# Half of the last half's convolution as matmuls, output blocks leaving from a key buffer, and a new order of the whole program

## The chip, the cores and the metric

The kernel runs on one core of one Trainium2 chip. The core has five engines with queues of their own: TensorE (PE), VectorE (DVE), ScalarE (ACT), GpSimd (POOL) and SyncE (SP), and 16 DMA engines. The metric is the device time in microseconds (us) of one execution; lower is better. The time before is the median of six runs.

## The reference

Block-sparse attention (blocks of 32, window, first and last block global, three random blocks a row), whose output is the input of a gated feed-forward layer with a depthwise convolution of three taps along the sequence. There are 4 batches of 768 tokens, 8 heads of 64, and a hidden width of 1024.

```python
scores = np.where(mask, scale * q @ k.T, -1e9)          # mask: window, global and sampled blocks
attn_out = softmax(scores) @ v                          # (4, 8, 768, 64) -> x (4, 768, 512)
h = np.maximum(x @ w_in, 0.0)                           # (4, 768, 1024)
hp = pad(h, one zero row at each end of the sequence)
for k in range(3):
    conv_out += conv_w[k][None, None, :] * hp[:, k:k + S, :]
gate = 1.0 / (1.0 + np.exp(-conv_out))
return h * gate @ w_out                                 # (4, 768, 512)
```

## The kernel before

**Halves and pairs.** The work is cut into eight halves `n`, each 384 tokens of one batch, and every half into four pairs of heads `hp`. For each pair, `attention` writes three score tiles into PSUM (two `st` tiles, L1003 to L1057), ScalarE takes the exponentials (L1021, L1046, L1064), one A.V step multiplies them with the values (67 matmuls, L1104), VectorE divides by the row sums (L1115, L1116), TensorE transposes (L1127), and ScalarE or VectorE copies the result into `xT` (L1134 or L1136).

**Feed-forward.** When all four pairs of a half are in `xT`, eight groups of four matmuls make x @ w_in (L1270, called f1 in what follows), each into one of four PSUM tiles `mix`; ScalarE or VectorE writes the relu into `hE` (L1281 or L1283). Two relu chunks make one convolution unit, so a half has four units, `a` = 0 to 3. A unit is done in one of two ways:

- `conv`, on VectorE: six taps (L1184), two adds (L1191), tanh on ScalarE (L1199), +1 (L1202), product with h into `gT` (L1211).
- `conv_pe`, on TensorE: six matmuls with diagonal matrices `dg` into an `st` tile (L1231), tanh on ScalarE straight from PSUM (L1240), +1 (L1243), product (L1246). Before, this is unit 2 of every half.

The diagonal matrices are made by GpSimd, six multiplications of the identity by a column of the taps (L687). A small patch (L1301 to L1308) mends the column where two halves of a batch meet.

**Output.** `out_block(n, c)` multiplies one third of a half's `gT` by w_out: eight matmuls of 512 columns in four pairs, one for each unit (L1154). One copy brings the block to a staging tile `o2s` (L1162 on ScalarE, L1164 on VectorE; three such tiles), and SP sends its 256 KB out (L1167). The third block of an even half waits for the patch, so it is written together with the odd half's blocks.

**Keys and values.** GpSimd issues the loads of q, k and v (L704, L791). Keys are transposed on TensorE (L733), evicted (L744, L746), and the sampled key blocks are copied into one of two key buffers `kg` (L913, VectorE and GpSimd). Values are rearranged on VectorE (L802) and written to a scratch tensor `vs` in DRAM by SP (L812); from there whole rows return into `vn` (L823) and the sampled rows into `vg`, by SP (L932) or by indirect DMAs of GpSimd (L923), eleven gathers a half. `vd` holds copies of the corner blocks of v (L842) and `kd` the global key blocks (L769).

**What sets the order.** Nothing above runs in the order of the source. Each step is an operation of a `Plan`: it has a priority (a due time), the engines that may do it with a cost each, its inputs, and the buffers that it takes from a pool or uses. `forward` builds an order for all five queues from these, `backward` makes new priorities from it, and `worth` gives the order a value by replaying it with jittered costs. `run` repeats this; it then changes the priorities at random, 200 times, and keeps the best order found. Which of two engines does an eviction is decided in the same search. The instructions are then written out in that order, and each engine works through its queue in turn.

Of the kernel before, what the change touches and what calls it, by code (L numbers as in the profile page):

```python
# [8 lines left out]
FP32 = mybir.dt.float32  # L9
# [60 lines left out]
PAGE, FETCH, FIRST = 256, 4.2, 63  # L70
LANES = 8
COLD_AFTER, COLD_FOR, REPLAYS = 2.2, 4.0, 6


class Plan:


    def __init__(self):
        self.ops = []
        self.pools = []  # L80

    def pool(self, n):
        p = Pool_(n)
# [3 lines left out]
    def op(self, alts, fn, prio, deps=(), lat=None, dma=None, mode=None, alloc=(), uses=(), earliest=0.0,  # L87
           after=(), lazy=False, n=0, nd=1, slack=0.0, gap=None):
        o = Op(alts, fn, prio, [d for d in deps if d is not None], lat, dma, mode, earliest)
        o.key = len(self.ops)  # L90
        o.lazy = lazy
        o.n = n
        o.nd = nd
        o.slack = slack
        o.gap = gap
        o.after = [d for d in after if d is not None]
        for b in alloc:
            o.allocs.append(b)
            b.users.append(o)
        for b in uses:  # L100
            o.uses.append(b)
            b.users.append(o)
        self.ops.append(o)
        return o
# [294 lines left out]
    def run(self, passes=6, trials=200):  # L399

        shake = random.Random(2)
        prio = [o.prio for o in self.ops]
        best = None
        for x in range(passes):
            order, span = self.forward(prio, x == 0)
            span = self.worth(order) if REPLAYS else span
            if best is None or span < best[0]:
                best = (span, list(prio), x == 0)
            prio = self.backward()
        for x in range(trials):  # L410
            prio = [p + shake.gauss(0.0, 1.0) for p in best[1]]
            for y in range(3):
                try:
                    order, span = self.forward(prio, False)
                except RuntimeError:
                    break
                span = self.worth(order) if REPLAYS else span
                if span < best[0]:
                    best = (span, list(prio), False)
                prio = self.backward()  # L420
        order, span = self.forward(best[1], best[2])
        return order
@with_exitstack
def kernel(
# [11 lines left out]
    nc = tc.nc  # L436
# [11 lines left out]
    QE, VE = 22.0, 34.0  # L448
    GAP, NGAP = 0.0, 1
    NSP = (5, 6, 7, 7, 7, 7, 7, 8)  # L450
    PEC = (2,)

    sb = ctx.enter_context(tc.tile_pool(name="sb", bufs=1))
    ps = ctx.enter_context(tc.tile_pool(name="ps", bufs=1, space=bass.MemoryType.PSUM))
# [72 lines left out]
    def t_act(n):  # L527
        return 0.07 + n / 1200.0
# [10 lines left out]
    def TS(s):  # L539
        return 12.0 + 2.5 * s if s < 4 else 22.0 + 5.0 * (s - 4)  # L540
# [603 lines left out]
    he_buf, he_m, gt_buf, gt_m, gate, relus = {}, {}, {}, {}, {}, {}  # L1144
    patch = {}

    def out_block(n, c, due, deps):
        b, g = divmod(n, 2)
        ob, mb = Buf(P_os), Buf(P_mix)
        prev = None  # L1150
        for a in range(4):
            def fn(e, a=a):
                for ffc in (2 * a, 2 * a + 1):
                    nc.tensor.matmul(out=mix_t[mb.index], lhsT=gT_t[gt_buf[n].index][:, ffc, 128 * c:128 * c + 128],  # L1154
                                     rhs=woutb[:, ffc, :], start=(ffc == 0), stop=(ffc == NFFC - 1),
                                     skip_group_check=True)
            prev = op({"PE": 2 * t_mm(512)}, fn, due + 0.2 * a, [prev, wout_ld[a // 2]] + deps[a], mode="F",
                      alloc=[mb] if a == 0 else [], uses=[gt_buf[n]] + ([mb] if a else []), n=4)

        def ev(e):  # L1160
            if e == "ACT":
                nc.scalar.copy(out=o2s_t[ob.index], in_=mix_t[mb.index])  # L1162
            else:
                nc.vector.tensor_copy(out=o2s_t[ob.index], in_=mix_t[mb.index])  # L1164
        evo = op({"ACT": t_act(512), "DVE": t_dps(512)}, ev, due + 1.5, [prev], alloc=[ob], uses=[mb])
        t0 = 384 * g + 128 * c
        sp(lambda e: nc.sync.dma_start(out=out[b, t0:t0 + 128, :], in_=o2s_t[ob.index]), due + 2.5, [evo], 0.75, uses=[ob], slack=0.0 if n == NHALF - 1 else 4.0)  # L1167

    last_cv = [None]
    last_mark = {}  # L1170
# [80 lines left out]
    for n in range(NHALF):  # L1251
# [12 lines left out]
        for ffc in range(NFFC):  # L1264
            hb = Buf(P_mix)
            due = base + W * 0.5 * ffc / 8

            def f1(e, ffc=ffc, hb=hb, n=n):
                for fc in range(NFC):
                    nc.tensor.matmul(out=mix_t[hb.index][:, 0:384], lhsT=winb[:, fc, 128 * ffc:128 * ffc + 128],  # L1270
                                     rhs=xT_t[xt_buf[n].index][:, fc, :], start=(fc == 0), stop=(fc == NFC - 1),
                                     skip_group_check=True)
            f_op = op({"PE": 4 * t_mm(384)}, f1, due, [win_ld[ffc // 4], he_m[b]] + [xtr[(n, hp)] for hp in range(4)], mode="F",
                      alloc=[hb], uses=[xt_buf[n]], n=8)

            def rl(e, ffc=ffc, hb=hb, b=b, g=g):
                dst = hE_t[he_buf[b].index][:, ffc, 1 + 384 * g:385 + 384 * g].rearrange(
                    "f (n r c) -> f n r c", r=4, c=8)
                src = mix_t[hb.index][:, 0:384].rearrange("f (n c r) -> f n r c", c=8, r=4)
                if e == "ACT":  # L1280
                    nc.scalar.activation(out=dst, in_=src, func=AF.Relu, bias=0.0, scale=0.5)  # L1281
# [78 lines left out]
```

## Time and profile before

| | us |
|---|---|
| median of six runs | 248.95 |
| range of the six runs | 247.27 to 252.5 |
| the profiled execution, its own time | 249.46 |
| its span in the profile | 247.6 |
| mean granted TensorE clock | 0.922 of full |

The page is one profiled execution: busy time of each engine, the span in 40 slices, the chain of work that ended last, and groups of instructions by source line. The time of the execution is 1.86 us longer than its span. Where the text speaks of a step of an instruction, it is the distance from one start to the next in an unbroken run of that instruction, which is shorter than the duration shown, because neighbours overlap.

### The profile page before, as it was taken

The numbers are of one execution on the slowest core, as the hardware profiler recorded it, in microseconds if no ns is written. First come the engines' busy times: TensorE is split into PE (matmuls) and PEld (weight loads), VectorE is DVE, ScalarE is ACT, GpSimd is POOL, SyncE is SP. The second block draws the span as 40 slices with busy tenths as digits, with TensorE's granted clock in tenths as the row PEclk, the third lists the DMA queues.
The fourth block names the chain that finished last, engine by engine and source line by source line (L and its number), as shares of the span: only waits on it lengthen the run. The fifth ranks groups of instructions, "written<-read, shape, count | busy, mean of one in ns | idle before, by whom it ended". The sixth has DMA issues, their size and how long they took to land.

```text
span 247.6 us, 10802 instructions
## 1 busy us (share of the span) xinstructions
PE 197.1 (80%) x4105; PEld 136.3 (55%) x4121; DVE 181.0 (73%) x657; ACT 171.9 (69%) x298; POOL 104.1 (42%) x203
## 2 busy tenths in 40 slices
PE   5233689497798499799869989699599999987792
PEld 1223577356465366668656755567376756645430
DVE  6545365378699958369998993769996984795882
ACT  8732858457578587779967985868587777865741
POOL 8068478870778791075388600753522000000000
PEclk9655758979999979999997999999999999999999
DMA  6949929999797369895519966674004412200113
GB/s 92 204 121 225 208 33 216 252 230 192 221 208 160 81 107 210 266 243 134 84 35 202 249 173 230 112 158 104 16 14 93 144 25 99 76 3 21 68 42 127
DMA packets 31687, 33.90 MB, mean 137 GB/s; under 512 B 4636, under 2 KB 27476, under 8 KB 31636
## 3 DMA queue, kind: packets, MB, share of 16 engines
q0 software_dynamic: 13600, 14.93, 35.3%
q1 hardware_dynamic: 17628, 17.89, 25.1%
q8 instruction: 32, 0.52, 0.9%
q10 hardware_dynamic: 408, 0.40, 0.6%
q14 instruction: 19, 0.16, 0.2%
HBM read 35.12 MB, written 9.62 MB: 181 GB/s over the span
## 4 chain that ended last, share of the span: by engine, by line
DVE 28%; PE 28%; DMA 13%; POOL 10%; issue 10%; ACT 6%; DVEq 1%; POOLq 1%; SPq 1%; ACTq 0%
PE mix L1154 10%; DVE m L1184 9%; DVE m L1191 5%; PE mix L1270 5%; POOL vg L923 5%; DMA vs<-vr 4%; PE mix L1104 3%; DMA vst<-in_v_dram 3%; DMA vg<-vs,idx 3%; DMA hE<-in_k_dram 3%; DVE xtok L1116 3%; PE st L1057 2%; DVE kg L913 2%; DVE gT L1211 2%; PE st L1039 2%
## 5 line engine op out<-in xcount | busy, mean ns | idle before, releaser
L1154 PE MATMUL mix<-woutb,gT 128*128 128x512 bf16 x176 | 45.6, 386 | 8.7 <-DVE gT L1211 5.7
L923 POOL DMA_INDIRECT vg<-vs,idx x34 | 33.9, 997 | 36.0 <-PE mix L1104 16.6
L1270 PE MATMUL mix<-xT,winb 128*128 128x384 bf16 x256 | 48.5, 341 | 0.5 <-DVE xT L1136 0.5
L1184 DVE TENSOR_SCALAR m<-hE,cw 128x384 bf16<-128x384 bf16 x144 | 36.0, 319 | 8.2 <-ACT hE L1281 8.1
L1281 ACT ACTIVATE hE<-mix 128x384 bf16<-128x384 f32 x56 | 27.7, 495 | 11.9 <-PE mix L1270 11.6
L1270 PEld LDWEIGHTS <-winb 128*128 128x128 bf16 x256 | 25.2, 101 | 16.8 <-issue 3.7
L913 DVE COPY kg<-kt 128x128 bf16 x192 | 26.6, 214 | 6.1 <-issue 6.0
L1046 ACT ACTIVATE pg<-st 128x736 bf16<-128x736 f32 x32 | 25.2, 788 | 7.7 <-PE st L1039 6.6
L1154 PEld LDWEIGHTS <-gT 128*128 128x128 bf16 x192 | 17.1, 99 | 23.5 <-DVE gT L1211 6.8
L1064 ACT ACTIVATE pr<-st 128x704 bf16<-128x704 f32 x32 | 24.4, 761 | 8.1 <-PE st L1057 7.8
L1104 PE MATMUL mix<-vg,pr 96*32 96x65 bf16 x704 | 26.3, 198 | 0.0
L1104 PE MATMUL mix<-vs,pa 128*32 128x65 bf16 (+1 forms) x320 | 25.8, 198 | 0.0
L1191 DVE TENSOR_TENSOR m<-m 128x768 bf16<-128x768 bf16 x48 | 25.6, 553 | 0.1
L913 POOL COPY kg<-kt 128x128 bf16 x72 | 20.4, 330 | 12.6 <-DVE kt L746 5.5
L1104 PE MATMUL mix<-vd,pg 128*32 128x130 bf16 x352 | 24.3, 227 | 0.8 <-POOL vd L842 0.8
L1199 ACT ACTIVATE m<-m 128x768 bf16<-128x768 bf16 x24 | 20.1, 848 | 5.2 <-DVE m L1191 5.1
L1104 PE MATMUL mix<-vn,pa 96*32 96x65 bf16 (+1 forms) x384 | 23.0, 199 | 0.0
L1104 PEld LDWEIGHTS <-pg 128*32 128x32 bf16 x736 | 21.5, 98 | 2.2 <-issue 1.5
L1104 PEld LDWEIGHTS <-pr 96*32 96x32 bf16 x704 | 21.6, 98 | 1.9 <-issue 1.6
L1104 PEld LDWEIGHTS <-pa 128*32 128x32 bf16 (+1 forms) x704 | 21.1, 97 | 2.4 <-issue 2.2
L1057 PE MATMUL st<-qb,kg 128*128 128x64 bf16 x352 | 16.8, 197 | 5.3 <-POOL kg L913 2.5
L1021 ACT ACTIVATE pa<-st 128x320 bf16<-128x320 f32 x32 | 14.0, 437 | 9.8 <-PE st L1012 8.8
(111 smaller groups left out, 420.0 us busy)
## 6 DMA issues: line engine op xcount, KB each, us to landing
out_dram<-o2s SPq DMA_DIRECT2D x24, 256.0 KB
vg<-vs SPq DMA_DIRECT2D x162, 32.5 KB
vn<-vs SPq DMA_DIRECT2D x8, 390.0 KB
vs<-vr SPq DMA_DIRECT2D x14, 195.0 KB
vst<-in_v_dram POOLq DMA_DIRECT2D x7, 384.0 KB, 7.4
nat<-in_k_dram POOLq DMA_DIRECT2D x12, 192.0 KB, 5.0
nat<-in_q_dram POOLq DMA_DIRECT2D x12, 192.0 KB, 4.8
winb<-in_moe_w_in_dram POOLq DMA_DIRECT2D x2, 512.0 KB
```

The lines of the kernel that those rows point to most:

```text
L913: eng.tensor_copy(out=dst[:, :, x, 32 * s:32 * s + 32], in_=KT[kt_buf[b].index][:, :, bass.ds(block_off(e, i0 + x, s, True), 32)])
L923: nc.gpsimd.indirect_dma_start(out=VG[vg_buf[n].index][:, x, :], out_offset=None, in_=vs_t[b][:, :], in_offset=bass.IndirectOffsetOnAxis(a ...
L1046: nc.scalar.activation(out=pg_t[pg.index], in_=st_t[sg.index][:, 0:736], func=AF.Exp, bias=0.0, scale=0.125)
L1057: nc.tensor.matmul(out=st[:, 64 * x:64 * x + 64].rearrange("p (h s) -> p h s", h=2), lhsT=kg[:, o:o + 128], rhs=qcol(i), start=True, stop= ...
L1064: nc.scalar.activation(out=pr_t[pr.index], in_=st_t[sr.index][:, 0:704], func=AF.Exp, bias=0.0, scale=0.125)
L1104: nc.tensor.matmul(out=dst, lhsT=l_, rhs=r_, start=(y == 0), stop=(y == len(lists[j]) - 1), skip_group_check=True)
L1154: nc.tensor.matmul(out=mix_t[mb.index], lhsT=gT_t[gt_buf[n].index][:, ffc, 128 * c:128 * c + 128], rhs=woutb[:, ffc, :], start=(ffc == 0), ...
L1184: nc.vector.tensor_scalar(out=mv(dst)[:, y], in0=hE_t[heb.index][:, f0 + y, c0 + tp_:c0 + tp_ + cn], scalar1=cw[:, tp_, f0 + y:f0 + y + 1] ...
L1191: nc.vector.tensor_tensor(out=m[:, 0], in0=m[:, 0], in1=m[:, x], op=ALU.add)
L1199: th = op({"ACT": t_act(W)}, lambda e: nc.scalar.activation(out=m_t[cb.index][:, 1], in_=m_t[cb.index][:, 0], func=AF.Tanh, bias=0.0, scal ...
L1270: nc.tensor.matmul(out=mix_t[hb.index][:, 0:384], lhsT=winb[:, fc, 128 * ffc:128 * ffc + 128], rhs=xT_t[xt_buf[n].index][:, fc, :], start= ...
L1281: nc.scalar.activation(out=dst, in_=src, func=AF.Relu, bias=0.0, scale=0.5)
```

## The change

Four things change. In the last half (`n` = 7) unit 3 also goes through `conv_pe`, so two of its four convolution units are matmuls; `dg` grows from six to twelve diagonal matrices, and GpSimd makes the second six in an operation that may not start before 130 on the planner's clock. The last four output blocks (three of half 7, and the third of half 6) are copied into a key buffer `kg` instead of `o2s`. The buffer is taken once, by a mark due when attention has ended, and each block has a 2 KB slot of it in every partition. The search of the order no longer adds a random number to the priority of all operations in a trial, but only to those whose priority lies in one stretch of 40 us, with a wider spread, from another seed; of 500 trials, 18 listed ones are worked out. The order of every queue comes out of that search, so it differs from before throughout the program.

```diff
+WIDTH, SIGMA = 40.0, 4.0
+SEED, TRIALS, KEEP = 1, 500, (0, 2, 5, 7, 11, 16, 27, 47, 48, 50, 81, 84, 95, 135, 197, 234, 350, 396)
...
-        shake = random.Random(2)
+        shake = random.Random(SEED)
...
-        for x in range(trials):
-            prio = [p + shake.gauss(0.0, 1.0) for p in best[1]]
-            for y in range(3):
+        for x in range(TRIALS):
+            lo = shake.uniform(-30.0, best[0])
+            prio = [p + shake.gauss(0.0, SIGMA) if lo <= p <= lo + WIDTH else p for p in best[1]]
+            for y in range(3 if KEEP is None or x in KEEP else 0):
...
-    PEC = (2,)
+    PEC = (2, 3)
+    ONPE = [(2,)] * 7 + [(2, 3)]
...
-        dg_ops[a_] = op({"POOL": 2.0}, mkdg, TS(3) + 0.1 * z, [cw_op, i_sel])
+        dg_ops[a_] = op({"POOL": 2.0}, mkdg, TS(3) + 0.1 * z if z == 0 else 120.0, [cw_op, i_sel], after=list(dg_ops.values()),
+                         earliest=0.0 if z == 0 else 130.0)
...
+    kg_late = Buf(P_kg)
+    kg_late_m = pl.mark(kg_late, TS(4 * NHALF))
+
     def out_block(n, c, due, deps):
         b, g = divmod(n, 2)
-        ob, mb = Buf(P_os), Buf(P_mix)
+        late = n == NHALF - 1 or (n == NHALF - 2 and c == 2)
+        ob, mb = kg_late if late else Buf(P_os), Buf(P_mix)
+        slot = c if n == NHALF - 1 else 3
+
+        def o2s():
+            if late:
+                return KG[ob.index][:, 1024 * slot:1024 * slot + 1024].bitcast(FP32)
+            return o2s_t[ob.index]
...
-                nc.scalar.copy(out=o2s_t[ob.index], in_=mix_t[mb.index])
+                nc.scalar.copy(out=o2s(), in_=mix_t[mb.index])
...
-        evo = op({"ACT": t_act(512), "DVE": t_dps(512)}, ev, due + 1.5, [prev], alloc=[ob], uses=[mb])
+        evo = op({"ACT": t_act(512), "DVE": t_dps(512)}, ev, due + 1.5, [prev] + ([kg_late_m] if late else []),
+                 alloc=[] if late else [ob], uses=[mb] + ([ob] if late else []))
...
-            if b not in WHOLE and ffc % 2 == 1 and ffc // 2 in PEC:
+            if b not in WHOLE and ffc % 2 == 1 and ffc // 2 in ONPE[n]:
                 conv_pe(n, ffc // 2, due + 1.5, relus[n][ffc - 1:ffc + 1])
```

More of the change, by code (lines that the diff above doesn't have):

```diff
@@ L80, in __init__ @@
         self.pools = []
+        self.kept = []
     def pool(self, n):
@@ L397, in worth, with run @@
         return sum(self.replay(order, random.Random(100 + x)) for x in range(REPLAYS)) / REPLAYS
-    def run(self, passes=6, trials=200):
-        shake = random.Random(2)
+    def run(self, passes=6):
+        shake = random.Random(SEED)
         prio = [o.prio for o in self.ops]
@@ L419, in run @@
                     best = (span, list(prio), False)
+                    self.kept.append(x)
                 prio = self.backward()
@@ L1161, in ev @@
             if e == "ACT":
-                nc.scalar.copy(out=o2s_t[ob.index], in_=mix_t[mb.index])
+                nc.scalar.copy(out=o2s(), in_=mix_t[mb.index])
             else:
-                nc.vector.tensor_copy(out=o2s_t[ob.index], in_=mix_t[mb.index])
-        evo = op({"ACT": t_act(512), "DVE": t_dps(512)}, ev, due + 1.5, [prev], alloc=[ob], uses=[mb])
+                nc.vector.tensor_copy(out=o2s(), in_=mix_t[mb.index])
+        evo = op({"ACT": t_act(512), "DVE": t_dps(512)}, ev, due + 1.5, [prev] + ([kg_late_m] if late else []),
+                 alloc=[] if late else [ob], uses=[mb] + ([ob] if late else []))
         t0 = 384 * g + 128 * c
-        sp(lambda e: nc.sync.dma_start(out=out[b, t0:t0 + 128, :], in_=o2s_t[ob.index]), due + 2.5, [evo], 0.75, uses=[ob], slack=0.0 if n == NHALF - 1 else 4.0)
+        sp(lambda e: nc.sync.dma_start(out=out[b, t0:t0 + 128, :], in_=o2s()), due + 2.5, [evo], 0.75, uses=[ob], slack=0.0 if n == NHALF - 1 else 4.0)
     last_cv = [None]
```

## The prediction, written before the changed kernel was run

> **What bounds the kernel now.** I read the page's totals first: is one engine full?
>
> ```profile
> PE 197.1 (80%) x4105; PEld 136.3 (55%) x4121; DVE 181.0 (73%) x657; ACT 171.9 (69%) x298; POOL 104.1 (42%) x203
> ```
>
> None is, so the order on the queues sets the time. The chain that ended last agrees; TensorE and VectorE have equal shares:
>
> ```profile
> DVE 28%; PE 28%; DMA 13%; POOL 10%; issue 10%; ACT 6%; DVEq 1%; POOLq 1%; SPq 1%; ACTq 0%
> ```
>
> Next, stages. The first w_in product (L1270) of a half is a milestone: it starts at 48.6 us for half 0, 106.9 for half 2, 164.6, 187.6, 211.0 and 227.1 for halves 4, 5, 6, 7 (the L1270 instructions by window). Busy time between the last of these:
>
> ```profile
> 187.60:211.00 23.40, 22.85 (x479) 15.82 (x477) 16.69 (x57) 18.50 (x34) 0.35 (x1) 1.00 0.32 95
> 211.00:227.10 16.10, 13.89 (x293) 9.01 (x293) 14.41 (x43) 10.39 (x19) 0.00 (x0) 1.00 0.06 20
> 227.10:243.60 16.50, 13.99 (x72) 6.78 (x71) 11.62 (x39) 9.72 (x17) 0.00 (x0) 1.00 0.12 48
> ```
>
> Columns after the length: PE, PEld, DVE, ACT, POOL, clock, DMA. Half 5's stage is TensorE alone (22.85 of 23.40); after 211 it is not full. The chain there is VectorE's convolution:
>
> ```profile
> 229.79 2.85 DVE m L1184 x12
> 232.64 1.40 DVE m L1191 x3
> ...
> 237.26 1.38 DVE m L1184 x6
> ...
> 239.61 0.57 DVE m L1191
> ...
> 240.20 0.85 ACT m L1199
> ...
> 241.47 0.57 DVE gT L1211
> ...
> 242.09 1.48 PE mix L1154 x6
> ```
>
> TensorE waits for gates; VectorE itself once waited long for relus:
>
> ```profile
> DVE m L1184 <- ACT hE L1281: 3.2, 1, 3.2
> PEld L1154 <- DVE gT L1211: 3.0, 4, 1.3
> ```
>
> No row has an output copy waiting for a staging buffer's DMA: ACT's L1162 waits only for L1154.
>
> **The Trainium skill.** "VectorE: DVE Perf Modes", section on the perf-mode tier table, puts bf16 tensor_scalar in a 4x mode and tensor_tensor in 2x. The trace agrees in kind: a 384-wide tap steps at 1.38/6 = 0.23 us, a 768-wide add at 0.47. "TensorE: Matmul & The Clock Gate", section on the HAM clock gate, says that an idle array falls to half clock and needs about 3.4 us of work to recover. The trace agrees: eleven L1057 take 0.74 us at 25.6 us and 0.48 at 38.8, so a new hole costs TensorE twice. "Perfetto Trace Analysis", section on identifying performance opportunities, says bottlenecks change between regimes; the table above does that.
>
> **The change, part by part.**
>
> *Third convolution unit of half 7 to TensorE.* Removed on VectorE: six taps, 1.38, and two adds, 2 x 0.47: 2.3 us of queue time. The +1 (L1243 for L1202) and gate product stay; ACT's tanh from PSUM is 0.81 instead of 0.85. Added on TensorE: six L1231, which step at the 0.163 us of L1270 (32 in 5.2 us): 1.0 us. It needs a score tile; both are free, attention being over.
>
> *Six more diagonal matrices on POOL.* 6 x 0.71 = 4.2 us, placed behind half-5 input loads, with part of those loads and two rounds of value gathers behind it. Taken as 0 to +1.5 us; I use 0, since POOL is 42% busy and input loads there run well ahead.
>
> *Last four output blocks in a key buffer.* Same copy (0.59 on ACT, 0.69 on VectorE), same 256 KB, same SP issue (0.37). No present wait is removed and the key buffer was last read long before: nothing, -0.3 to +0.3. After the last copy (244.23) the end at 247.6 stays 3.4 us away.
>
> *New order.* Every queue changes, so this is most of the risk. By the changed program's order, VectorE takes five more of the 24 output copies, and six value-corner copies (0.22 each) come from POOL. Net of the other moves VectorE gets about +1.8 us of work, ACT +0.3, TensorE +1.0. SP sends the first vn load ahead of the first three gathers (each 0.37 of issue) and not behind them; three key evictions move to ACT at the start (0.80 there, 0.56 on VectorE); both hide in ACT's wait until 22.4 for the first q transposes (8.1). Three stages I worked through:
>
> (a) Start. The first two A.V products need all eleven gathers of half 0. Now POOL issues its six at 20.3 to 28.2, a kd copy behind them waits until 32.24 for them to land, and A.V starts at 33.2. After: all four q loads come first, five gathers run from about 20.9 to 27, then a vd copy waits for those five (about 31.3), and only then the sixth is issued, landing some 3.5 to 4.8 later (the present one 4.8): 35.5 to 37. Behind that vd copy on POOL stand the sixth gather, another vd copy, both w_in loads (0.8 each), nine key copies (2.2) and the v loads of batch 1. A.V starts about 3 us late, and cold. But VectorE's normalisation of pair 3 now stands behind a copy that waits for a v load until 46.38, and TensorE idles 3.24 us before 48.07. That load is now issued at 38.4; after, at 31.3 + 0.5 (vd) + 1.3 (gather) + 0.5 (vd) + 1.7 (w_in) + about 0.5 (register work) + 2.2 (key copies) + 1.3 (one gather of half 1, now behind it) = 39.3, with the w_in transfers a us ahead of it and earlier than now. So it lands within about a us of now, and A.V's 3 us fit into this hole: f1 of half 0 moves by -0.5 to +1.5; I use +0.3.
>
> (b) Half 5's stage, full on TensorE. Counting matmuls at their steps (L1270 0.163, L1154 0.215, an A.V set of 67 0.85, an L1057 set 0.32, an L1008 to L1039 score set 0.75) gives 22.2 us now and 21.0 after: one A.V set and one score set have left. Half 4's stage gets 2.3 more, but has 3 idle; half 3's gets 2.0 less. I take -1.2, from -2.5 to +2.
>
> (c) Halves 6 and 7, from 211.0 to the last matmul at 243.6: 32.6 us now. I walked the new order by hand with the durations above. Half 6's 32 L1270 with one score set (5.2 + 0.75) and half 7's first A.V (0.85) make 6.8. From that point: A.V sets of pairs 1 and 2 (to 1.7), L1231 x6 (2.7), L1057 (3.0), exponential on ACT 0.76 (3.8), A.V of pair 3 (4.8). VectorE does four adds first (to 3.6), two xT copies, and normalises pairs 2 and 3 at 0.75 each with a +1 of 0.3 between (6.05); transposes and xT copy follow (0.35 + 0.5): half 7's f1 can start at 6.95. Half 6's last output blocks hold two of four mix banks, so relus pace L1270: the third relu on ACT stands behind a tanh that waits for VectorE's second add of half 6's last unit (10.65), and comes at 12.0. With 16 L1154 ahead of and between them, half 7's f1 ends at 15.7; L1231 x12 end at 17.7 (16.6 is the last relu). Then 32 L1154 x 0.215 = 6.9 run nearly without a hole (gates at 17.6, 19.1, 20.1, 21.0), to 24.9 with 0.3 of gaps. 6.85 + 24.9 = 31.7: -0.9. The 2.3 us taken from VectorE don't all come out, since **TensorE is late next**: it issues all 32 last L1154 after half 7's convolutions. The walk has no stall for instruction fetch: -2 to +1.5.
>
> Sum: +0.3 - 1.2 - 0.9 = -1.8. The profiled execution took 249.46, 1.86 more than its span of 247.6, so it becomes 247.7. It stands 0.5 above the median of the six runs (248.95); from the median, 247.15.
>
> **Rivals.** 0.5% is 1.25 us, about what a measurement of this kernel can tell from no change.
>
> *A, likeliest: TensorE's stages get shorter, as summed.* For: half 5's stage has no slack, and both walked stages end sooner. Against: counted by these steps TensorE works 158 of the 195 us from 48.6 to 243.6, so 37 us are holes, which a new order can fill or widen. 247.2; own range 245.0 to 248.5.
>
> *B, the end gains in full.* If the order also closes VectorE's 3.2 us wait for relus and TensorE's 3.7 us for gates (the waits of 211 to 244 have L1154 wait 2.1 us for L1211 and 1.6 for L1308), the unit's 2.3 us come out whole beside (b), with up to 1.5 more: 248.95 - 1.2 - 2.3 - 1.5 = 244. Against: the 6.9 us block of L1154.
>
> *C, slower: the sixth gather.* The vd copy on POOL holds that gather back. It decides once it lands later than about 37: the 3.2 us hole before 48.07 is then used up, and winb, v loads and later gathers behind it on POOL move too. Landing at 39 with a cold array: +2 in (a), and what POOL loses returns in the half-2 gathers, where the chain lies on it (62 to 79 us): +1 to +2. Less 1.2 for (b): 251. For: its slot is behind a drain of five gathers. Against: q loads and vn arrive sooner.
>
> *D, no change.* VectorE's extra 1.8 us of output copies, in stages where it is near TensorE (21.9 of 24.1 us from 106.9 to 131), eat the gain: 248.95 - 1.8 + 1.8 = 249.
>
> *E, the change doesn't do what it says.* The order does show twelve L1231 ahead of the last L1154 and four copies into kg, so only the size is open.
>
> **Chances.** A 0.40, B 0.17, C 0.23, D and E 0.20. Of A some 0.08 ends within 0.5%; of D about 0.06 ends slower and 0.03 faster. Faster: 0.32 + 0.17 + 0.03 = 0.52; slower 0.23 + 0.06 = 0.29; within 0.5%: 0.19. The time is A's 247.2. The range reaches down to B's 244 and its unknown (b), 243.5, and up to C's 251.
>
> **What would show it.** Right: f1 of half 0 starts within 1.5 us of 48.6; the stage from half 5's f1 to half 6's is about 22 us; from half 6's f1 to the last matmul about 31.7; L1231 runs 54 times, L1184 138; the last 32 L1154 stand without holes over 0.5 us. Wrong: f1 of half 0 after 50.5 (C); half 5's stage not shorter; VectorE still last on the chain before the final L1154 (gate later than the 26th of 32). Over 249 with both walked stages shorter means the loss is in halves 1 to 4, which I only counted.

## The result and the profile after

The changed kernel takes **249.24 us** (median of 26 runs, 245.26 to 252.41); the kernel before, run beside it on the same chip, 251.01 (55 runs, the six of the table above among them). The ratio is **0.9909, interval [0.9876, 0.9941]**: 0.9% faster, 2.3 us of 251. It is made from the fast runs alone, those within 1.5% of the fastest of their kernel, so it is not quite the ratio of the two medians, 0.9930. The prediction's 247.15 for 248.95 was a ratio of 0.9928. The sign and the size were right. One of its two gains was not where it was put.

Two profiles of the changed kernel are used. In the first one (its execution took 250.98 us) half 4's stage ran at a granted clock of 0.88, so figures for the whole span come from the second (248.36 us, span 246.6). The last three stages are shown from the first, since TensorE had full clock there, as it had before. Lines moved with the edits: f1 is L1288 (was L1270), the w_out matmul L1171 (L1154), taps L1202 (L1184), adds L1209, relu L1299, gate L1229, diagonal matmul L1249 (L1231), an A.V product L1111 (L1104), the last scores L1064 (L1057) with their exponential L1071, normalisation L1122 and L1123, transposes L1134.

First the page of the second profile, totals and then the chain by engine:

```profile
PE 197.0 (80%) x4108; PEld 136.3 (55%) x4127; DVE 184.2 (75%) x661; ACT 171.6 (70%) x294; POOL 103.9 (42%) x201
...
PE 52%; DVE 18%; DMA 10%; issue 7%; ACT 4%; SPq 3%; POOL 2%; POOLq 1%; DVEq 1%; ACTq 0%
```

TensorE's and VectorE's shares of the chain were equal, 28% each; now TensorE alone has half of it. VectorE's busy time did not fall: eight instructions left in half 7, but the output and corner copies that moved there more than replace them, and the same 192 copies into `kg` took 28.6 us where they took 26.6.

Busy time by stage, first profile: half 5, half 6, half 7, each from its first f1 product to the next (the last to the end of the last matmul). Columns after the length are PE, PEld, DVE, ACT, POOL, clock, DMA share, GB/s:

```profile
190.86:212.08 21.22, 21.01 (x388) 14.03 (x391) 17.21 (x56) 16.99 (x32) 0.00 (x0) 1.00 0.24 65
212.08:228.75 16.67, 12.92 (x354) 9.12 (x352) 10.38 (x34) 10.04 (x18) 0.00 (x0) 1.00 0.13 50
228.75:245.57 16.82, 16.77 (x88) 8.51 (x87) 13.09 (x43) 9.36 (x17) 0.00 (x0) 1.00 0.17 63
```

| stage | before | after | change |
|---|---|---|---|
| half 5 | 23.40 | 21.22 | -2.2 |
| half 6 | 16.1 | 16.67 | +0.6 |
| half 7, to the last matmul | 16.5 | 16.82 | +0.3 |

Half 5's stage has 91 matmuls fewer and is still TensorE alone (21.01 of 21.22). Half 7's is now full too (16.77 of 16.82; it was 13.99 of 16.50). All of the slack left in the last 33 us stands in half 6's stage: 3.75 us. It is read in the waits of that stretch of the first profile (in total, times, longest):

```profile
DVE m L1202 <- ACT hE L1299: 5.3, 1, 5.3
...
PE mix L1111 <- issue: 1.6, 1, 1.6
```

Two lines stand out. VectorE waits 5.3 us for a relu before half 6's taps. The kernel before had no such wait there; its wait of 3.2 us stood ahead of half 7's taps, and that one is gone. VectorE's queue before:

```profile
213.02 1.46 DVE L1184 TENSOR_SCALAR m<-hE,cw 128x384 bf16<-128x384 bf16 x6
...
229.79 2.39 DVE L1184 TENSOR_SCALAR m<-hE,cw 128x384 bf16<-128x384 bf16 x10 [3.18 <-ACT hE L1281]
```

So half 6's taps began 2.0 us after half 6's f1, and now begin 6.7 after it. And TensorE stands 1.6 us before an A.V product with no wait at all ("issue"). The chain of the first profile, in order of time (start, length, what), goes through only one of the two:

```profile
216.28 1.97 PE mix L1288 x12
...
218.26 0.50 ACT hE L1299
...
218.79 2.84 DVE m L1202 x12
...
223.03 1.87 DVE m L1209 x4
...
226.53 0.56 DVE xtok L1123
...
227.35 0.48 DVE gT L1229
...
236.71 1.95 PE st L1249 x12
...
238.71 6.87 PE mix L1171 x31
```

From half 6's last f1 product it is the last relu, twelve taps, adds and normalisations on VectorE, and then half 7's f1. After that there is TensorE alone, up to 31 output matmuls in 6.87 us without a hole.

### The profile page after: what moved, and what is told of

Same layout as the page of the kernel before. It is cut to its first block, busy times and chain, and to the rows that moved or that the text cites. A ratio compares the mean times of both kernels' runs of the same rounds, so it can differ in the third digit from the quotient of the medians.

```text
span 249.2 us, 10788 instructions
## 1 busy us (share of the span) xinstructions
PE 199.3 (80%) x4108; PEld 138.4 (56%) x4127; DVE 183.3 (74%) x661; ACT 171.6 (69%) x294; POOL 105.2 (42%) x201
## 4 chain that ended last, share of the span: by engine, by line
PE 46%; DMA 16%; DVE 14%; issue 8%; POOL 6%; SPq 4%; ACT 3%; POOLq 1%; DVEq 0%
PE mix L1171 12%; PE mix L1288 12%; PE mix L1111 6%; DMA vn<-vs 4%; DMA vst<-in_v_dram 3%; PE st L1064 3%; DMA vg<-vs,idx 3%; DMA out_dram<-o2s 3%; DMA hE<-in_v_dram 3%; PE st L1046 2%; DVE m L1202 2%; DVE xtok L1123 2%; PE st L1249 2%; POOL vg L930 2%; PE st L1019 2%
## 5 line engine op out<-in xcount | busy, mean ns | idle before, releaser
L1171 PE MATMUL mix<-woutb,gT 128*128 128x512 bf16 x173 | 47.6, 395 | 2.4 <-DVE gT L1229 1.1
L1288 PE MATMUL mix<-xT,winb 128*128 128x384 bf16 x256 | 45.4, 326 | 0.8 <-ACT qb L766 0.4
L1202 DVE TENSOR_SCALAR m<-hE,cw 128x384 bf16<-128x384 bf16 x138 | 35.8, 326 | 8.3 <-ACT hE L1299 7.9
L1071 ACT ACTIVATE pr<-st 128x704 bf16<-128x704 f32 x32 | 24.2, 758 | 21.9 <-PE st L1064 21.8
L1299 ACT ACTIVATE hE<-mix 128x384 bf16<-128x384 f32 x55 | 27.0, 494 | 11.1 <-PE mix L1288 10.6
L1288 PEld LDWEIGHTS <-winb 128*128 128x128 bf16 x256 | 24.6, 98 | 16.8 <-issue 1.1
L1111 PE MATMUL mix<-vg,pr 96*32 96x65 bf16 x704 | 27.8, 201 | 4.7 <-DMA vg<-vs,idx 2.2
L920 DVE COPY kg<-kt 128x128 bf16 x192 | 27.9, 227 | 0.7 <-DVE kt L753 0.3
L1111 PE MATMUL mix<-vs,pa 128*32 128x65 bf16 (+1 forms) x320 | 27.5, 202 | 1.1 <-issue 0.9
L1171 PEld LDWEIGHTS <-gT 128*128 128x128 bf16 x192 | 17.6, 101 | 15.7 <-DVE gT L1229 1.7
L1111 PE MATMUL mix<-vd,pg 128*32 128x130 bf16 x352 | 24.8, 232 | 0.7 <-POOL vd L849 0.7
L1209 DVE TENSOR_TENSOR m<-m 128x768 bf16<-128x768 bf16 x46 | 24.5, 548 | 0.2
L1111 PEld LDWEIGHTS <-pg 128*32 128x32 bf16 x736 | 22.1, 100 | 4.3 <-issue 3.4
L1111 PEld LDWEIGHTS <-pa 128*32 128x32 bf16 (+1 forms) x704 | 21.9, 99 | 4.4 <-issue 3.8
L1111 PE MATMUL mix<-vn,pa 96*32 96x65 bf16 (+1 forms) x384 | 24.2, 202 | 0.0
L1111 PEld LDWEIGHTS <-pr 96*32 96x32 bf16 x704 | 22.2, 100 | 3.2 <-issue 2.3
L1064 PE MATMUL st<-qb,kg 128*128 128x64 bf16 x352 | 17.9, 200 | 5.1 <-DVE kg L920 2.5
L1123 DVE TENSOR_TENSOR xtok<-mix,rcp 128x384 bf16<-128x384 f32 x32 | 17.8, 557 | 5.1 <-PE mix L1134 4.1
L1064 PEld LDWEIGHTS <-kg 128*128 128x128 bf16 x352 | 15.6, 102 | 10.8 <-DVE kg L920 3.2
```

Source lines behind the costliest of these rows:

```text
L920: eng.tensor_copy(out=dst[:, :, x, 32 * s:32 * s + 32], in_=KT[kt_buf[b].index][:, :, bass.ds(block_off(e, i0 + x, s, True), 32)])
L1064: nc.tensor.matmul(out=st[:, 64 * x:64 * x + 64].rearrange("p (h s) -> p h s", h=2), lhsT=kg[:, o:o + 128], rhs=qcol(i), start=True, stop= ...
L1071: nc.scalar.activation(out=pr_t[pr.index], in_=st_t[sr.index][:, 0:704], func=AF.Exp, bias=0.0, scale=0.125)
L1111: nc.tensor.matmul(out=dst, lhsT=l_, rhs=r_, start=(y == 0), stop=(y == len(lists[j]) - 1), skip_group_check=True)
L1123: nc.vector.tensor_tensor(out=xtok_t[xk.index], in0=o_[:, :, :, 0:64], in1=rcp.unsqueeze(3).broadcast_to([128, 3, 2, 64]), op=ALU.mult)
L1202: nc.vector.tensor_scalar(out=mv(dst)[:, y], in0=hE_t[heb.index][:, f0 + y, c0 + tp_:c0 + tp_ + cn], scalar1=cw[:, tp_, f0 + y:f0 + y + 1] ...
```

## Experiments

Twelve runs follow. The changed kernel again, the one with unit 3 back on VectorE and the two with chunks in order ran on one chip with the kernel before (median 251.3 of 59 runs there). The unit alone in the old order, the two with moved boundaries and the one with the moved A.V product ran on a second chip (kernel before 272.83, 44 runs), and the last four on a third (272.05, 12 runs). On the two slower chips half 0's f1 alone starts 4 to 8 us later. Whole times are therefore compared only as ratios to the kernel before on the same chip, and stages only where the clock in the row is the same.

### The changed kernel again

> The changed kernel once more, unaltered, for a second profiled execution and as the base of the runs beside it. Both theories: 0.985 to 0.996 of the kernel before. In its profile the first w_in product of half 6 should start some 21.2 us after that of half 5 (it did so in the first profile) and the last w_out matmul should end 33 to 34 us after half 6's first product, not the 31.7 of my walk, because half 6's eight products come in a shuffled order of chunks.

Measured: 249.45 us (22 runs), ratio 0.9906 [0.9867, 0.9946]. Half 5's stage is 21.22 again. Halves 6 and 7 take 17.49 and 17.56 at clocks of 0.95 and 0.96. The 5.3 us and the 1.6 us waits return to the tenth. From half 0's f1 to half 5's it took 138.7 us, where the first profile had 142.1 and the kernel before 139.0: these five stages vary by 3 us from run to run, and nothing under that is read from one profile of them.

### Half 7's unit 3 back on VectorE, in the new order

```diff
+        dve = n == NHALF - 1 and a_ == 3
...
+            if dve:        # six taps, two adds on VectorE where the six matmuls stood
+                ...
+                return
```

> The changed kernel with its third unit of half 7 back on VectorE: where its six diagonal matmuls stood, six taps and two adds run on VectorE (into tiles of the attention that are free by then), and the tanh reads them; everything else stands as it was. Theory 1 (the unit's move is worth something because VectorE's gates let the last w_out block start): gates come 2.3 us later, TensorE has 1.0 us less to do, so the end comes 1.3 to 2.0 us later. Theory 2 (the end is TensorE's 32 last matmuls, so the move buys nothing and the new order is all): 1.0 us sooner to 0.3 later.

Measured: 251.81 us (22 runs), ratio 1.0052 [1.0013, 1.0091]. The changed kernel has 0.9906, so undoing this one part costs 1.5% by the two ratios, about 3.7 us, and 2.4 us by the two medians (249.45 and 251.81). The new order, which was searched with these matmuls in it, is slower without them than the old order. Half 5's stage keeps its 21.2. The difference is all in half 7:

```profile
209.43:226.12 16.69, 12.95 (x355) 9.11 (x352) 10.39 (x34) 10.03 (x18) 0.00 (x0) 1.00 0.13 50
226.12:246.71 20.59, 17.64 (x82) 8.24 (x81) 15.49 (x50) 9.51 (x17) 0.00 (x0) 0.92 0.14 52
```

and its chain shows how (the taps and adds of the unit are L1251 and L1255 here):

```profile
234.97 1.38 DVE pa L1251 x6
236.35 0.48 DVE pa L1255
...
237.41 0.48 DVE gT L1229
237.94 0.39 PE mix L1171
238.38 8.34 PE mix L1171 x30
```

A gate that stands behind the added taps and adds on VectorE is ready at 237.9, and all 31 output matmuls wait for it; TensorE idles 2.89 us there. The stage is 3.8 us longer, in two equal parts. The output matmuls start 11.8 us into it and not 10.0, and then take 8.8 us where they took 6.9. The granted clock goes with the second part: it is 0.58 in the 4.06 us from 237.94, right behind the hole, and 1.00 before and after. The expected 1.3 to 2.0 covers the first part alone; the direction was right.

### Only that unit on TensorE, in the old order

```diff
+                if late:          # taps and adds of half 7's unit 3
+                    return
...
+                if n == NHALF - 1:    # behind the patch of half 7
+                    ... six matmuls with a second set of diagonal matrices
```

> The kernel before in its own order, with only unit 3 of half 7 changed: its six taps and two adds leave VectorE, and six matmuls with a second set of diagonal matrices take their place on TensorE, put out right behind the patch of half 7; GpSimd makes the second six matrices when half 6's first unit starts. Theory 1 (TensorE's and VectorE's queues in the last two stages set the end, and the new order is needed to use the freed time): the last matmul comes 0.5 to 1.5 us sooner (243.56 in the kernel before), 1.1 us by a walk of the last gates; the changed kernel's other gain, in half 5's stage, is missing, so it stands between the two kernels. Rival O (the new order does it all, and the unit alone brings nothing or a loss, as TensorE's six matmuls take what VectorE saves): 0 to +1 us.

Measured: ratio 0.9997 [0.9922, 1.0072]; an effect of 1 us is inside that interval. The profile tells more, since these stages are at full clock as before:

```profile
234.33:250.45 16.12, 13.97 (x293) 9.01 (x293) 14.41 (x43) 10.33 (x19) 0.00 (x0) 1.00 0.06 20
250.45:265.95 15.50, 14.78 (x78) 7.45 (x77) 9.27 (x31) 9.59 (x17) 0.00 (x0) 1.00 0.13 51
```

Half 6 as before to the hundredth, half 7 in 15.50 and not 16.5: the last matmul comes 0.9 to 1.0 us sooner for half 7's f1, where a walk had said 1.1. So the unit is worth 1 us in the old order and 2.4 to 3.7 in the new one: unit and order belong together. It also shows that the new order is *not* better in halves 6 and 7: 31.6 us here, 33.5 in the changed kernel.

### Half 6's chunks in the order in which they are needed

The search shuffles the eight f1 chunks of a half. In half 6 they now come as 7, 2, 4, 1, 5, 6, 3, 0, before as 0, 1, 3, 2, 4, 5, 7, 6; unit 0, which VectorE does first, needs chunks 0 and 1. The edit names chunks by the place at which their relu is put out:

```diff
-    ... lhsT=winb[:, fc, 128 * ffc:128 * ffc + 128],
+    ... lhsT=winb[:, fc, 128 * FM[n, ffc]:128 * FM[n, ffc] + 128],
...
+                FM[n, ffc] = done[n] if n in (6,) else ffc
+                done[n] += 1
```

> The changed kernel with one thing altered: in half 6, whichever of the eight products runs k-th makes chunk k, so the first convolution unit on VectorE has its two relus first instead of last. Order and engines of all instructions stay. Theory 1 (the walk was wrong only in taking the chunks in order; VectorE's 5.3 us of idle time before half 6's first taps holds up normalisation of half 7's pairs behind it): the end comes 1.5 to 2.5 us sooner, ratio to the unaltered changed kernel about 0.992. Theory 2 (TensorE's own work sets the end, VectorE's wait costs nothing): within 0.3 us.

Measured: 247.83 us (6 runs, too few for a ratio). The stage is 16.20 and not 16.67, then 16.82 as before it:

```profile
211.87:228.07 16.20, 12.89 (x354) 9.12 (x352) 10.69 (x34) 9.95 (x18) 0.00 (x0) 1.00 0.14 51
228.07:244.89 16.82, 16.76 (x88) 8.51 (x87) 13.10 (x43) 9.37 (x17) 0.00 (x0) 1.00 0.17 63
```

VectorE's wait of 5.3 us is gone, but only 0.5 us comes out. The chain shows what took its place:

```profile
218.02 2.17 PE mix L1111 x145
220.19 1.62 issue
221.81 0.51 PE mix L1111 x19
```

It now runs through TensorE, and the 1.6 us without a wait are on it.

### The chunks of all halves in order

The same edit with `range(NHALF)` in place of `(6,)`.

> The changed kernel with the same alteration in all eight halves: the relu that is written r-th in a half is that of chunk r, so that the units find their relus as early as the order allows. Theory 1: the 1.5 to 2.5 us of half 6 and up to as much again from halves 1, 2, 3 and 5, whose chunks are shuffled too: 2 to 4 us sooner than the unaltered changed kernel. Theory 2: within 0.3 us.

Measured: 248.65 us (22 runs), ratio 0.9940 [0.9903, 0.9977]: not told apart from the changed kernel's 0.9906 (249.45 us). Half 6's stage is 16.20 again, so the 0.5 us are there, but the whole time does not show them. The expected size was far off: the mixed order in the other halves costs nothing that can be measured.

### What the 1.6 us are

The hole lies inside the third of three A.V products in a row, some 360 of their 402 instructions in (each product is 67 matmuls with as many weight loads). The Trainium skill, "Runtime: NRT & Kernel Launch", section "Instruction fetch mechanics", says that engines stream their instructions in blocks of 16 KiB, 256 instructions, fetched by DMA, and that a boundary is mostly hidden. The DMA queues of the first profile show that stream from 216 to 224 us: two packets, 0.03 MB, on a queue of their own.

```profile
q8 instruction: 2, 0.03, 1.5%
```

Its count in a whole run fits blocks of 256. TensorE has 8,300 instructions in the changed kernel, 32.4 blocks, and the page has 32 packets; in the kernel further down with 192 more, 33.2 blocks, it has 33.

I counted TensorE's instructions from the program and put every 256th beside the trace of the second profile. The planner has the same idea, in the kernel before too: with `PAGE, FETCH, FIRST = 256, 4.2, 63` it counts TensorE's instructions in blocks of 256 and lets a block begin no sooner than 4.2 us after the step that entered the one before it, so the search weighed such stalls. The boundaries are the numbers that leave 193 when divided by 256, as all seven below do. From 40 us on, TensorE stood over 0.2 us without a wait seven times, and each time at such a boundary:

```
instruction  reached at us  after the boundary before  hole ahead of it
       1729        62.1                   6.3               4.0
       3009       101.6                   5.2               1.2
       3265       105.9                   4.3               0.7
       4801       144.8                   6.7               0.2
       5313       156.4                   5.9               0.5
       6081       170.5                   1.9               0.3
       7873       217.9                   3.2               1.65
```

The waits say the same of the largest ones (second profile):

```profile
PE st L1249 <- issue: 4.0, 1, 4.0
PE mix L1111 <- issue: 3.4, 4, 1.6
```

So the page's block size agrees with the trace, and "mostly hidden" fails where 256 short instructions come faster than the next block: two A.V products are 268 instructions in 1.6 us, and the block that was waited for at 217.9 came 3.2 us after the one before. (Only at 6081 was a block there after 1.9 us; while the DMA queues were busy, at 62.1, one took 6.3.) The first profile has six such holes at boundaries, and one of 0.22 us that is at none. Two kernels test it that only move the boundaries: more warm-up matmuls of 16 columns at the start, where TensorE is idle.

```diff
     nc.tensor.matmul(out=mix_t[1], lhsT=warm[:, 0:128], rhs=warm, ...)
+    for _ in range(12):      # six in the other kernel; eight calls
+        nc.tensor.matmul(out=mix_t[1][:, 0:16], lhsT=warm[:, 0:128], rhs=warm[:, 0:16], ...)
```

> The changed kernel with 96 more matmuls of 16 columns among the first eight warm-up products, in a stretch in which TensorE has nothing else to do; all that follows is as before, only 192 instructions (matmuls and weight loads) later in TensorE's stream. Theory F (TensorE's instructions come in blocks of 256, and one block needs at least 3.2 us after the one before it, more when the DMA queues are full): the holes without a wait move to other places. From the times of the single matmuls in the profile, with 4.5 us a block up to 200 us and 3.25 after, they sum to 6.5 us and not 9.9 (0.7 and not 1.8 us after 186), so the kernel becomes 1 to 3 us faster. Rival (these holes are something else, or lie beside other waits): 0 to +0.5 us for the added matmuls.

> As the kernel with 96 more matmuls, with 48 of them, so 96 instructions later in TensorE's stream. Theory F: by the same sum the holes become 19.7 us and not 9.9 (4.4 and not 1.8 us after 186), at about 60, 103, 117, 150, 164, 177, 191, 205 and 227 us; since not all of them lie on the path, the kernel becomes 3 to 9 us slower. Rival (the holes are something else): 0 to +0.3 us.

Measured, on one chip: 192 instructions later, 267.13 us (22 runs), ratio 0.9857 [0.9804, 0.9910]; 96 later, 276.21 us (6 runs), ratio **1.0270 [1.0112, 1.0428]**. The same work in the same order differs by 4%, some 9 us by the medians and 11 by the ratios, and the kernel with *fewer* added matmuls is the slower one. The two expectations together ask for 4 to 12. Gaps of over 0.3 us at the boundaries, start to start, sum to 1.6 us in the first and 11.8 in the second; in the second they stand at 45, 64, 108, 112, 164, 176, 222, 243 and 247 us of a run that is some 25 us longer. That is the count of holes that was expected, several at its places. Half 0's f1 starts at 53.4 and 53.55 us, so the difference arises behind the added matmuls, and in stages that have holes: half 0's is 3.25 us longer with 2.1 us of idle time at a boundary (at a clock of 0.93 and not 1.00), half 1's 3.1 longer with 3.2, half 5's, full on TensorE, 1.55 longer with 1.4. In half 3's stage 2.4 us of it cost only 0.45. The rival, that these holes are something else or all stay beside other waits, is out for these two. The changed kernel was not run on that chip, so how much either place brings or costs against it is open.

The boundaries are not the only place where TensorE stands without a wait on this chip and the third one. The profiles there show 14 to 30 more such holes each, 6 to 13 us in all and most of 0.5 us, away from any boundary; the two profiles of the changed kernel on the first chip have one, of 0.2 us. They come in rows, 0.75 us apart, as here in the kernel with the sixth gather early (below):

```profile
124.60 0.22 PE L1111 MATMUL mix<-vd,pg 128*32 128x130 bf16 x1 [0.50 <-issue]
...
125.36 0.24 PE L1111 MATMUL mix<-vg,pr 96*32 96x65 bf16 x3 [0.50 <-issue]
...
126.13 0.19 PE L1111 MATMUL mix<-vn,pa 128*32 128x65 bf16 x1 [0.51 <-issue]
```

What they are is open. The two shifted kernels have about 10 us of them each, so they don't make the difference between these.

### One A.V product moved out of the row

```diff
+        av = next(o for o in order if o.key == 838)     # A.V of half 7, pair 2
+        order.remove(av)                                # to behind the last scores of pair 3
+        order.insert(next(x for x, o in enumerate(order) if o.key == 846) + 1, av)
```

> The changed kernel, with one step moved on TensorE: the A.V product of pair 2 of half 7 stands behind the six diagonal matmuls of half 6 and the last scores of pair 3, not ahead of them, so that two A.V products stand in a row and not three. Theory F (in the last stages TensorE stands 1.6 us inside the third of three A.V products in a row, with no wait shown; about 400 short instructions come there in 2.3 us, and the next block of instructions is not there yet): the hole of 1.6 us goes or shrinks to under 0.5 us, the first f1 product of half 7 comes 0.8 to 1.4 us sooner after that of half 6 (16.7 us in the changed kernel at full clock, so 15.3 to 15.9), and the time falls by 0.5 to 1.4 us. Rival S (half 6's chunks come in a mixed order, so VectorE's taps start late, and VectorE sets the start of half 7's f1): no change within 0.5 us, since VectorE's queue is as it was.

Measured: ratio 0.9801 [0.9602, 1.0000] (6 runs). The hole is gone from the boundary at instruction 7873, but the stage is not shorter:

```profile
225.65:243.13 17.48, 13.83 (x354) 9.46 (x352) 11.19 (x37) 10.15 (x18) 0.00 (x0) 0.94 0.13 48
```

17.48 at a clock of 0.94, against 17.49 at 0.95 in the changed kernel run again. The rival was right: as the kernel stands, VectorE sets the start of half 7's f1, and the hole beside it is free.

### Both edits at once

> The changed kernel with both edits for half 6's stage: half 6's chunks are made in the order in which VectorE's units need them, and the A.V product of pair 2 of half 7 stands behind the six diagonal matmuls and the last scores. Theory 2 (half 7's f1 starts when the later of two chains ends: VectorE's, which starts late because of the mixed chunks, and TensorE's, with the 1.6 us hole inside three A.V products; each edit alone only uncovers the other chain): from half 6's f1 to half 7's is 14.7 to 15.4 us at full clock (16.7 in the changed kernel, 16.2 with sorted chunks alone), from half 6's f1 to the last matmul 31.5 to 32.3 (33.5 in the changed kernel), and the time falls by 1.2 to 2 us against the changed kernel on the same chip. Rival (a third thing sets this start, the last scores' exponentials on ScalarE or the normalisation of pair 3): 16.2 as with sorted chunks alone, and no more than 0.5 us.

Measured: ratio 0.9697 [0.9617, 0.9776]; the changed kernel beside it on that chip has 0.9734 [0.9657, 0.9811]. The times can't tell them apart; the stage can:

```profile
224.66:240.31 15.65, 13.05 (x355) 9.30 (x353) 10.67 (x34) 10.17 (x18) 0.00 (x0) 1.00 0.14 53
```

Half 6's stage falls from 16.67 to 15.65, by 1.0 us, where the chunks alone gave 0.5 and the A.V product alone nothing. Two chains end nearly together and hide each other. The expected 14.7 to 15.4 was missed by 0.25, and the chain says why: the boundary has not gone, it has moved into the product that was moved.

```profile
234.62 0.58 issue
235.19 0.69 PE mix L1111 x36
```

### Both edits, with the boundaries moved

As the shifted kernels, with 14 matmuls in each of the eight calls.

> The kernel with both edits, and 112 more matmuls of 16 columns among the warm-up products, so that all that follows stands 224 instructions later in TensorE's stream. Theory F (blocks of 256 instructions, each at least 3.2 us after the one before): by the sum over the blocks this place leaves the fewest holes without a wait, about 4 us and not 8 to 10 in all, so it is 1 to 3 us faster than the kernel with both edits. Rival (the holes lie beside waits that stay): within 0.5 us of it.

Measured: ratio 0.9708 [0.9626, 0.9790], no different from 0.9697. Its gaps at the boundaries sum to 1.9 us, but those of the unshifted kernel came to only 2.4 in its profile, not to the 8 to 10 that the sum over blocks gave. The expectation failed with its premise: there was little left to take. The profile of the changed kernel on the same chip has 10.8 us by the same sum, and its time is not told apart either. The place does not settle the sum: at the boundary at 62 to 68 us, which these kernels reach by the same instructions, TensorE idled 4.0 us in the second profile, 1.25 in the changed kernel here and 0.1 in the one with both edits. And the holes away from boundaries make up for it: 6.4 us in the changed kernel here, 13.4 in the one with both edits. So the sum over one profile does not rank places; the 4% between 96 and 192 rests on the times of all their runs.

### The sixth gather early, the output blocks in staging tiles

```diff
+        order.remove(last)                   # GpSimd's sixth gather of half 0
+        order.insert(order.index(vd), last)  # ahead of the first vd copy
...
-                return KG[ob.index][:, 1024 * slot:1024 * slot + 1024].bitcast(FP32)
+                return o2s_t[LATE.setdefault(slot, len(LATE) % NOS)]
```

> The changed kernel with two parts undone that lie 200 us apart, so that the profile tells each by its stage: GpSimd's sixth gather of half 0 is put ahead of the copy that holds it back, and the last four output blocks leave from the three staging tiles again, the fourth using the tile of the first once its transfer is done. Theory of the prediction: the early gather brings 0 to 0.3 us before half 0's f1 (its start at 48.0 to 48.8 us), since the later load of v sets that start; the staging tiles cost 0 to 0.6 us between the last matmul and the end, by the wait of the fourth copy for the first transfer. Rival C: half 0's f1 comes 1 to 2 us sooner. Rival for the buffer: the last copy waits for a transfer of 2 us or more, and the end comes 1.5 us or more later after the last matmul.

Measured: ratio 0.9720 [0.9605, 0.9835]. GpSimd's queue in this kernel; the sixth gather is the one at 27.73:

```profile
27.73 0.91 POOL L930 DMA_INDIRECT vg<-vs,idx  x1 [0.30 <-issue]
31.52 0.85 POOL L849 COPY vd<-vn 32x260 bf16<-32x260 bf16 x2 [2.89 <-DMA vg<-vs,idx]
...
38.53 1.41 POOL L798 DMA_DIRECT2D vst<-in_v_dram  x2
```

The gather left 3.7 us sooner than in the changed kernel on that chip (31.46), the v load behind it only 0.3 us sooner (38.84 there). Half 0's f1 began at 55.98; it began at 52.77, 56.47 and 55.78 in the three kernels that shared the chip and had the gather late. No gain is seen. But the run doesn't test what covers the gather: on this chip VectorE waited for A.V products and not for the v load ahead of that f1, and the A.V products of half 0 began at 36.5 to 37.7 with and without the edit, with no wait for a gather. For the first chip the trace of the second profile has both waits, the one on TensorE at 36.1 us and the other on VectorE at 46.0:

```profile
36.10 0.21 PE L1111 MATMUL mix<-vg,pr 96*32 96x65 bf16 x1 [1.85 <-DMA vg<-vs,idx]
```

```profile
46.00 0.74 DVE L809 COPY vr<-vst 96x2048 bf16<-96x2048 bf16 x1 [1.81 <-DMA vst<-in_v_dram]
```

There the v load is the later of the two. From the last matmul to the end it is 3.7 us here, against 3.6 in the changed kernel on the same chip, so the key buffer is worth 0.1 us at most.

### The changed kernel on the third chip

> The changed kernel as it is, beside the others on this chip: ratio to the kernel before 0.988 to 0.994, as in its first runs.

Measured: 262.56 us (6 runs), ratio 0.9734 [0.9657, 0.9811]: more than on the first chip, and outside what was expected. The kernel before has no profile there. The old order with the one unit on TensorE has one on the second chip: 155.8 us from half 0's f1 to half 5's, against 150.6 and 151.6 in two kernels with the new order, and 158.4 in the one whose boundaries were moved by 96 instructions. On the first chip that stretch is the same for both orders, within its 3 us. So why the change brings more on the third chip is open; one profile of each kernel can't tell.

## Why the prediction was right, and where it was not

- **Start, +0.3.** Right. Half 0's f1 began at 48.7 and 48.0 (48.6 before). The sixth gather was held back as worked out: GpSimd waited for gathers to 31.5 (31.3 was said) and issued it at 32.3, A.V waited for it until 36.1 (35.5 to 37), and the v loads were issued at 38.65 (39.3). VectorE's wait for the v load, until 46.0, swallowed it, but only just: pair 3's A.V product also ended at 46.0, and it had ended at 43.9 before. Rival C is out on this chip.
- **Half 5's stage, -1.2.** Right in kind, low by 1.0: -2.2. The term that failed is the count of before. The counted 21.0 for after met 21.22, but the counted 22.2 for before stood against a measured 23.40, and the difference was taken between two counts and not from the measured stage. Of the 2.2, 1.84 are TensorE's busy time (22.85 to 21.01), 0.34 its idle time. The two stages ahead of it, counted at -2.0 and +2.3, went further the same way: half 3's from 34.0 to 28.6, half 4's from 23.0 to 27.8 (second profile).
- **Halves 6 and 7, -0.9.** Wrong: +0.9, 33.5 us for a walked 31.7. Half 7's own part was walked too long (18.0, measured 16.82); half 7's f1 was walked to 13.75 us after half 6's and came at 16.67. Two things were missing in the walk. It took half 6's chunks in their order of number, so that VectorE had its twelve taps behind it when f1 ended; they start there, 2.84 us of queue time. And it gave no time to the instruction blocks: "the walk has no stall for instruction fetch" stood in the text with a range, and the stall is 1.6 us. The kernel with sorted chunks shows the one uncovering the other, the kernel with both edits gets back 1.0 of the 2.9 us. The rest isn't settled: 0.6 of it is the block boundary that moved along, for the other 1.3 no run was made. Rival B's condition was met in one part: the 3.2 us wait for relus closed, but the longer one in half 6 came in its place.
- **The unit on TensorE.** TensorE was late next, as said: 31 output matmuls in 6.87 us stand last. Its worth inside the order was not a term of the sum; it is 1 us in the old order and 2.4 to 3.7 in the new. The added matmuls step as costed: twelve in 1.95 us, 0.163 each.
- **Second diagonal set.** 4.2 us on GpSimd were taken; six took 6.1 (at 140.6 us in the second profile). No wait on the page names them, so zero was right.
- **The key buffer: nothing.** Right, 0.1 us. But the end moved for another reason. From the last matmul it was 4.08 us before and is 3.63 in both profiles, from the last copy 3.4 and 3.0, and the staging tiles in the new order leave 3.66. The last two copies start 1.3 us apart and no longer 0.5, so the new order is behind it; by which wait is not shown.
- **VectorE's added copies (rival D).** Its busy time rose by 3.2 us (181.0 to 184.2; 2.3 in the first profile), not by 1.8; 2.0 of it are the unchanged copies into `kg`, which took longer. In the stages from half 0's f1 to half 5's, where they should have told, the second profile has 138.7 us against 139.0. D is not seen, within the 3 us by which that stretch varies.
- **The sum.** -2.2, +0.9 and the end's -0.45 make -1.7 beside a start within 0.6; the measured ratio is -2.3, from -1.5 to -3.1. About half a us of the gain is therefore not placed, and the interval doesn't ask for it. It would have to lie in halves 0 to 4, which were only counted, and one profile of those can't show it.

The likeliest case was named rightly, "TensorE's stages get shorter", but one of the two walked stages got longer. The -1.8 came near -2.3 partly by luck: the count for half 5 was too small by 1.0, the walk for halves 6 and 7 too good by 1.8, and the end's 0.45 was not in the sum.

## What to carry to other kernels

When a walk through a new order gives a gain, take the order inside a group from the program and not from the source: here eight interchangeable chunks were shuffled, and the unit that was needed first got its data last. Where a wait has no releaser on the page, count the engine's instructions: on the first chip all but one of these holes stood at a block boundary, every 256th instruction, where short instructions had outrun their own delivery, and then the order of steps matters by how many instructions it puts side by side. On the other two chips most stood elsewhere, so the count has to be made and not assumed. Before one of two long waits is removed, see in the chain whether the other ends within half a microsecond of it; only both together moved this stage.

## What was not expected of the hardware

- TensorE's delivery of instructions is a resource with a price. In the last stages a block of 256 for which TensorE waited came 3.2 us after the one before, at 62 us 6.3. Moving all boundaries by 96 instructions made a kernel 4% slower than moving them by 192, with less work and in the same order.
- Two chips ran the kernel before in 272 to 273 us and the first in 251, 8% apart, and the change's ratio went from 0.991 to 0.973. The profiles from the two slower ones show rows of holes of 0.5 us on TensorE, without a releaser and away from the block boundaries, that the first chip's don't.
